# Chunked attention and two feed-forward networks in one kernel: blocks of 512 tokens, attention in quarters of the array, early conversion of the second network's weights

## The chip, the cores and the metric

One core of a Trainium2 chip runs the whole program in one launch. The metric is the device time in microseconds (us), the median of the runs shown. The profile is one execution; its span goes from the first to the last instruction.

## The reference

What is computed, in order (q, k, v have 8 batches, 8 heads, 576 positions, 64 channels; there are 4608 tokens, d_model is 512, d_ff 2048):

```python
# attention inside chunks of 64 positions
scores = q_c @ k_c.T / 8;  attn = exp(scores - max);  attn /= sum(attn) + 1e-9
x  = (attn @ v_c), heads side by side: [4608, 512]
h  = x @ w_in1;   x2  = relu(h)**2 @ w_out1
h  = x2 @ w_in2;  g = (a0 + a1 h + a2 h^2 + a3 h^3) / (1 + |b0||h| + |b1|h^2 + 1e-6)
out = g @ w_out2
```

The four weight matrices come as float64, everything else as float32.

## The kernel before, in words

Tokens run along the free axis. Every float32 operand of the networks is split exactly into two float32r parts, hi and lo, and every product is made of three passes, lo\*hi + hi\*lo + hi\*hi (`mm3`, L159 to L163; L161, L162 and L163 are the three passes). Tokens are cut into 12 blocks of NB = 384, d_ff into 16 chunks of 128. A **step** is one block with one chunk: the product into d_ff (`mm_h`, L165, 12 matrix instructions of 384 columns, into a tile h), the activation, and, LAG = 3 steps later, the product out of that chunk (`mm_out1`, L172, or `mm_out2`, L179) into four accumulators ACC in PSUM. The first network's product out has weights as the stationary operand (12 instructions of 384 columns, named acc<-gh,w and acc<-gl,w in the profile); the second's has the activations as the stationary operand and streams the weights (9 instructions of 512 columns, acc<-w,gh and acc<-w,gl; for the last four chunks acc<-wx,...). The first network's output goes to DRAM (x2d) and comes back for the second.

The first network's activation (`act1`, L200) is Relu and Square on ScalarE, then gh (a copy) and gl (a difference) on VectorE. The second's (`e1` to `e4`, L401 to L441) has six operations on ScalarE, six on VectorE, and gl on GpSimd.

**Attention** works on tiles of 128 tokens with all heads, and is woven into the first network's steps for the block after. Scores (`mm_s`, L276) and outputs (`mm_pv`, L286) are float32 products on halves of the array's columns, two at a time, 8 products of 128 columns (16 instructions in the trace) each. For that KP holds k with zeros for the other head of a pair, and AT the transposed probabilities with zeros for the other chunk. Between them VectorE takes maximum, difference, sum, reciprocal, product (`s_max`, `s_norm`) and one transpose in 32x32 blocks (`s_tr`, L318), whose pieces eight DMAs put into AT. The output leaves PSUM in `x_evac` (L329), a copy on ScalarE and a difference on VectorE. The q and k of the first nine tiles are transposed by TensorE (`tr_nat`), of the others by VectorE (`tr`, L241) from loads of 192 tokens. PSUM holds four accumulators, two h tiles and two tiles a for attention.

**Weights** come as float64 words and are made float32 on the chip (`w_words` on ScalarE, L128; `w_join` and `w_sign` on VectorE, L135 and L140), then split (`w_split`, L145: hi on ScalarE or VectorE, lo on GpSimd). A half is one chunk of one matrix, 128x512. The second network's weights take the slots of the first's when the last block is done with them, so their loads and their conversion lie in that block's steps and in the next.

**The order of the work.** Each event is put down by `at(time, ...)`, with the time in steps, and `issue` (L87) issues them in order of time, so every engine's queue has that order. Up to 14.5 steps the framework's own scheduler may reorder them (`in_order=False`, L554); from there on the order is as written. Each engine works its queue strictly in order. The constants of the order:

```python
n_ahead = 6                                             # L496: w_in halves ahead of the first step
w_get(-1.2 + 0.58 * j, 4.2, w_in1, w_out1, f, half, ...)  # L501: the other 26
start.append(NF * b - 8.6 - (TPB - 1 - i) * NF / TPB)   # L483: attention of tile i of block b
t0 = max(t, t0 + 0.5)                                   # L518: a second-network half every 0.5 step
```

Of the kernel before, what the change touches and what calls it, by code (L numbers as in the profile page):

```python
# [9 lines left out]
F32 = mybir.dt.float32  # L10
F32R = mybir.dt.float32r
# [8 lines left out]
NB = 384          # tokens of a block  # L20
UNIT = 192        # tokens of a load of q and k
LAG = 3           # steps from a product into d_ff to the product out of it
LN_SHIFT = 20     # Ln sees Q * 2**-LN_SHIFT
# [3 lines left out]
def attn_moe_moe_kernel(  # L27
# [37 lines left out]
    NAT = 3 * TPB     # tiles whose q and k the tensor engine transposes  # L65
# [6 lines left out]
    acc_p = ctx.enter_context(tc.tile_pool(name="acc", bufs=1, space=PSUM))  # L72
# [4 lines left out]
    ACC = [acc_p.tile([128, 512], F32, name=f"acc{i}", tag=f"acc{i}") for i in range(4)]  # L77
    x2d = [dram_p.tile([128, KC, NB], F32, name=f"x2d{b}", tag=f"x2d{b}") for b in range(NBLK)]
    co = const.tile([128, 8], F32, name="co")
    P = {}            # pools of the segment that is issued  # L80
    T = {}            # tiles on their way
# [5 lines left out]
    def issue(until, in_order=True):  # L87
        events.sort(key=lambda e: e[:2])
        with tc.manual_schedule() if in_order else nullcontext():
# [505 lines left out]
```

## Time and profile before

| | us |
|---|---|
| median of 3 runs | 1792.72 |
| lowest, highest | 1791.61, 1794.39 |
| profiled execution: span | 1790.2 |
| TensorE matrix instructions busy | 1727.4 (96%) |
| VectorE busy | 1197.0 (67%) |
| ScalarE busy | 1002.2 (56%) |
| GpSimd busy | 376.1 (21%) |
| chain that ended last: TensorE's share | 86% |

The profiled execution's span is 2.5 us below the median of the runs. The span of an instruction on TensorE includes time in its pipeline, so that 0.34 us of one overlaps the next; the distance from start to start is what an instruction costs. DVE is VectorE, ACT ScalarE, POOL GpSimd, SP the queue that issues the DMAs; PEld are the loads of the stationary operand, which overlap PE. A group's name is output<-inputs by the program's tile names.

### The profile page before, as it was taken

The page shows a single profiled execution, that of the slowest core. Times are in us where ns is not written, and L with a number is a line of the kernel's source. Part 1 is how long each engine was busy: PE and PEld are TensorE (multiplying, and loading weights), DVE is VectorE, ACT ScalarE, POOL GpSimd, SP SyncE. Part 2 cuts the span into 40 slices and gives each one's busy share as a digit, 9 for nine tenths or more (in the row PEclk, how much of TensorE's full clock was granted, in tenths as well). Part 3 has the DMA queues.
Part 4 walks back from the last instruction along what each step waited for, and adds up shares of the span by engine and source line. Part 5 has one row for each costly group of instructions (what it writes and reads, how often), then busy time and mean ns, then how long its engine had stood idle before and what let it go on. Part 6 is the DMA issues. An engine that isn't in the chain of part 4 may idle for free.

```text
span 1790.2 us, 26938 instructions
## 1 busy us (share of the span) xinstructions
PE 1727.4 (96%) x9888; PEld 1606.5 (90%) x9888; DVE 1197.0 (67%) x2117; ACT 1002.2 (56%) x1893; POOL 376.1 (21%) x343
## 2 busy tenths in 40 slices
PE   6789999999999999999986999999999999999998
PEld 5689999999999999999976999998989889889887
DVE  6994444444454444544599888888878878887876
ACT  6653222222222222222466888888787888888876
POOL 3540000000000000000386332332332322322322
PEclk9999999999999999999999999999999999999999
DMA  7654132232222322211453010000010000010000
GB/s 186 191 159 83 38 64 53 43 69 49 56 54 43 69 55 48 59 38 42 141 165 128 14 36 25 12 36 24 13 36 24 12 36 24 13 36 18 18 19 18
DMA packets 224484, 100.62 MB, mean 56 GB/s; under 512 B 183136, under 2 KB 214112, under 8 KB 224352
## 3 DMA queue, kind: packets, MB, share of 16 engines
q1 hardware_dynamic: 224352, 98.90, 21.0%
q8 instruction: 78, 1.28, 0.3%
q14 instruction: 54, 0.44, 0.1%
HBM read 71.31 MB, written 18.87 MB: 50 GB/s over the span
## 4 chain that ended last, share of the span: by engine, by line
PE 86%; DVE 8%; issue 4%; ACT 1%; DMA 1%; SPq 0%; POOL 0%; DVEq 0%; POOLq 0%; ACTq 0%
PE h L161 14%; PE acc L161 14%; PE h L162 14%; PE h L163 14%; PE acc L163 13%; PE acc L162 13%; DVE st L137 2%; PE a L283 2%; DVE wc L142 2%; PE a L292 2%; DVE gh L101 1%; DVE t L406 0%; DVE t L426 0%; DVE g L432 0%; DVE ev L101 0%
## 5 line engine op out<-in xcount | busy, mean ns | idle before, releaser
L161 PE MATMUL h<-x,w 128*128 128x384 f32 x1536 | 523.1, 341 | 28.6 <-ACT r L204 19.8
L162 PE MATMUL h<-x,w 128*128 128x384 f32 x1536 | 518.0, 337 | 0.3 <-DVE x L104 0.3
L163 PE MATMUL h<-x,w 128*128 128x384 f32 x1536 | 517.7, 337 | 0.0
L101 DVE CAST gh<-r 128x384 fp32r<-128x384 f32 x192 | 77.5, 404 | 391.1 <-PE acc L163 337.4
L161 PEld LDWEIGHTS h<-x,w 128*128 128x128 f32 x1536 | 290.1, 189 | 47.1 <-ACT r L204 20.9
L204 ACT ACTIVATE r<-h 128x384 f32<-128x384 f32 x192 | 93.7, 488 | 400.6 <-PE h L163 366.9
L104 POOL TENSOR_TENSOR gl<-g,gh 128x384 fp32r<-128x384 f32 x192 | 195.4, 1017 | 566.9 <-ACT gh L99 527.5
L162 PEld LDWEIGHTS h<-x,w 128*128 128x128 f32 x1536 | 290.0, 189 | 9.5 <-DVE x L104 0.7
L163 PEld LDWEIGHTS h<-x,w 128*128 128x128 f32 x1536 | 289.8, 189 | 0.2 <-issue 0.2
L161 PE MATMUL acc<-gh,w 128*128 128x384 f32 x768 | 262.5, 342 | 3.6 <-DVE ev L101 2.1
L163 PE MATMUL acc<-gh,w 128*128 128x384 f32 x768 | 259.2, 337 | 0.0
L162 PE MATMUL acc<-gl,w 128*128 128x384 f32 x768 | 259.0, 337 | 0.0
L406 DVE SCALAR_TENSOR_TENSOR t<-h,co,t 128x384 f32<-128x384 f32 x192 | 139.6, 727 | 124.5 <-ACT t L405 123.0
L104 POOL TENSOR_TENSOR gl<-r,gh 128x384 fp32r<-128x384 f32 x16 | 20.7, 1296 | 761.7 <-DVE gh L101 761.7
L161 PE MATMUL acc<-w,gl 128*128 128x512 f32 x432 | 171.3, 397 | 2.1 <-DVE ev L101 2.1
L162 PE MATMUL acc<-w,gh 128*128 128x512 f32 x432 | 171.0, 396 | 0.0
L163 PE MATMUL acc<-w,gh 128*128 128x512 f32 x432 | 170.7, 395 | 0.0
L161 PEld LDWEIGHTS acc<-gh,w 128*128 128x128 f32 x768 | 144.7, 188 | 10.2 <-issue 5.9
L163 PEld LDWEIGHTS acc<-gh,w 128*128 128x128 f32 x768 | 145.0, 189 | 0.0
L413 ACT ACTIVATE r<-t,co 128x384 f32<-128x384 f32 x192 | 118.6, 618 | 46.7 <-DVE t L406 29.0
L162 PEld LDWEIGHTS acc<-gl,w 128*128 128x128 f32 x768 | 144.6, 188 | 0.0
L99 ACT ACTIVATE gh<-g 128x384 fp32r<-128x384 f32 x192 | 100.9, 525 | 75.4 <-DVE g L432 75.4
(83 smaller groups left out, 2659.5 us busy)
## 6 DMA issues: line engine op xcount, KB each, us to landing
st<-in_moe_w_in_dram SPq DMA_DIRECT2D x32, 512.0 KB, 3.9
st<-in_moe_w_out_dram SPq DMA_DIRECT2D x32, 512.0 KB, 3.7
x2d<-ev SPq DMA_DIRECT2D x48, 192.0 KB, 2.0
x<-x2d SPq DMA_DIRECT2D x12, 768.0 KB, 4.3
out_dram<-ev SPq DMA_DIRECT2D x36, 256.0 KB, 2.0
at<-et SPq DMA_DIRECT2D x264, 32.0 KB, 1.8
v<-in_v_dram SPq DMA_DIRECT2D x32, 256.0 KB, 3.2
qs<-in_q_dram SPq DMA_DIRECT2D x288, 24.0 KB, 1.8
```

The lines of the kernel that those rows point to most:

```text
L99: nc.scalar.activation(out=o, in_=x, func=ACTF.Copy)
L101: eng.tensor_copy(out=o, in_=x)
L104: eng.tensor_tensor(out=o, in0=x, in1=hi.bitcast(F32), op=ALU.subtract)
L137: nc.vector.scalar_tensor_tensor(out=st[:, :, 0], in0=c, scalar=3, in1=st[:, :, 0], op0=ALU.logical_shift_left, op1=ALU.bitwise_or)
L142: nc.vector.scalar_tensor_tensor(out=c, in0=st[:, :, 1], scalar=-2 ** 31, in1=st[:, :, 0], op0=ALU.bitwise_and, op1=ALU.bitwise_or)
L161: nc.tensor.matmul(out=o, lhsT=al, rhs=bh, start=first and i == 0, stop=False)
L162: nc.tensor.matmul(out=o, lhsT=ah, rhs=bl, start=False, stop=False)
L163: nc.tensor.matmul(out=o, lhsT=ah, rhs=bh, start=False, stop=last and i == len(pairs) - 1)
L204: nc.scalar.activation(out=r, in_=ps, func=ACTF.Relu)
L283: nc.tensor.matmul(out=o[sl, p], lhsT=q_[:, p, sl], rhs=k_[:, p, c], start=True, stop=True)
L406: nc.vector.scalar_tensor_tensor(out=t, in0=h2, scalar=co[:, 5:6], in1=t, op0=ALU.mult, op1=ALU.add)
L413: nc.scalar.activation(out=r, in_=u, func=ACTF.Ln, scale=2.0 ** -LN_SHIFT, bias=co[:, 6:7])
```

## The change

Blocks have 512 tokens (nine blocks, four tiles each), so all matrix instructions of the networks have 512 columns, and the second network's w_out chunks all live in W (the wx tiles go). Attention's products work on quarters of the array: 16 products of 64 rows, 64 stationary and 64 moving columns each, in the order of QUARTERS, with each pair of heads in two PSUM banks; KP, AT's zeros and E2 go. In the steady order VectorE's transposes write the transposed probabilities directly, in eight pieces, and no DMA does. TensorE transposes q, k and the probabilities of the first four tiles alone. The second network's weights are converted during blocks 1 to 7, one half per three steps, and kept as float32 in DRAM (w2d); in the last block they are loaded into their slots and split. All is issued in the written order. PSUM first holds h and three double banks for attention, then h, four accumulators and one double bank.

```diff
-NB = 384          # tokens of a block
+NB = 512
...
+    def w_keep(key):
+        _, f, half = key
+        nc.sync.dma_start(out=w2d[f][half], in_=T.pop(("wc",) + key).bitcast(F32))
...
+    def w2_load(f, half):
+        nc.sync.dma_start(out=w_slot(f, half)[1].bitcast(F32), in_=w2d[f][half])
+
+    def w2_split(f, half, eng):
+        hi, lo = w_slot(f, half)
+        x = lo.bitcast(F32)
+        copy(eng, hi, x)
+        split_lo(nc.gpsimd, lo, x, hi)
...
+    QUARTERS = ((0, 0), (1, 1), (0, 1), (1, 0))
...
+    def mm_s(t, tag="a"):
+        q_, k_ = T.pop(("q", t)), T.pop(("k", t))
+        o = banks(P["aps"].tile([128, 2, 512], F32, name="a", tag=tag))
         for p in range(HP):
-            for c in range(2):
-                sl = slice(64 * c, 64 * c + 64)
-                nc.tensor.matmul(out=o[sl, p], lhsT=q_[:, p, sl], rhs=k_[:, p, c], start=True, stop=True)
-        T["s", t] = o.rearrange("p a h j -> p (a h) j")
+            for h, c in QUARTERS:
+                nc.tensor.matmul(out=o[half(c), h, p], lhsT=q_[half(h), p, half(c)], rhs=k_[half(h), p, half(c)],
+                                 start=True, stop=True)
+        T["s", t] = o
...
+            for c, h in QUARTERS:
+                nc.tensor.matmul(out=o[half(h), c, p], lhsT=v_[half(c), 2 * p + h], rhs=a_[half(c), :, p, h],
+                                 start=True, stop=True)
...
-        x = tl("attn", [128, 2, H, 32], F32, "et")
-        nc.vector.transpose(out=x, in_=e.rearrange("p h (a j) -> p a h j", a=2))
+        a = T["a", t] = tl("attn", [128, 2, HP, 2, 32], F32, "at", f"at{t % 2}")
         for c in range(2):
             for ih in range(2):
                 for jh in range(2):
                     i0, j0 = 64 * c + 32 * ih, 64 * c + 32 * jh
-                    nc.sync.dma_start(out=AT[t % 2][j0:j0 + 32, c, ih], in_=x[i0:i0 + 32, jh])
...
+                    nc.vector.transpose(out=a[j0:j0 + 32, ih], in_=e[i0:i0 + 32, :, :, 32 * jh:32 * jh + 32])
...
+    def attention(t, t0):
+        at(t0 - 1.2, tr, t, "qs", "q")
+        at(t0 - 1.0, tr, t, "ks", "k")
+        at(t0 + 0.45, mm_s, t)
+        at(t0 + 0.65, s_max, t)
+        at(t0 + 0.95, s_exp, t)
+        at(t0 + 1.1, s_sum, t)
+        at(t0 + 1.4, s_norm, t, nc.vector)
+        at(t0 + 1.55, s_tr, t)
+        at(t0 + 0.5, load_tok, t, v, "v", f"v{t % 2}")
+        at(t0 + 3.45, mm_pv, t)
+        at(t0 + 3.7, x_evac, t, nc.vector)
...
+        start[t] = 0.5 + 3.6 * i if b == 1 else NF * (b - 1) - 2 + 4 * i
...
+    n_ahead = 4
...
+        w_get(-0.8 + 0.5 * j, 1.3, 0, f, half_, w_split, (nc.scalar, nc.vector)[j % 2])
...
-                at(s + LAG + 0.6 + 0.1 * c, evac1, s // NF, c)
...
+                at(s + LAG + 0.98 + 0.01 * c, evac1, s // NF, c)
+                at(s + LAG + 1.2 + 0.1 * c, store1, s // NF, c)
...
+    for j in range(2 * NF):
+        w_get(NF + 4.2 + 3.0 * j, 3, 1, j // 2, j % 2, w_keep)
     T_P2 = NS - NF - 0.1
...
+    for f in range(NF):
+        for half_, t in ((0, NS - NF + f + 0.6), (1, NS - NF + f + LAG + 0.95)):
+            at(t, w2_load, f, half_)
+            at(t + 2.1, w2_split, f, half_, (nc.scalar, nc.vector)[half_])
```

## Rows read from the trace of the kernel before

**Rows 1.** Stretches: start and end (us), busy us (instructions) by engine, PEclk, DMA share, GB/s

```profile
0.00:35.08 35.08, 21.32 (x152) 15.67 (x152) 19.37 (x35) 20.04 (x35) 12.88 (x23) 0.95 0.78 180
35.08:130.56 95.48, 78.16 (x484) 71.54 (x485) 91.35 (x131) 60.86 (x114) 46.23 (x32) 0.96 0.65 183
...
207.04:281.05 74.01, 74.01 (x482) 71.48 (x481) 34.34 (x70) 20.36 (x40) 0.00 (x0) 1.00 0.26 54
...
871.89:957.00 85.11, 70.37 (x386) 67.77 (x385) 76.38 (x81) 52.97 (x99) 63.26 (x43) 0.98 0.52 170
957.00:1036.50 79.50, 70.52 (x346) 64.00 (x347) 70.01 (x109) 60.02 (x115) 33.62 (x28) 0.96 0.13 46
...
1237.50:1305.00 67.50, 67.24 (x337) 60.60 (x336) 54.33 (x98) 54.36 (x103) 20.17 (x20) 1.00 0.07 24
1710.10:1790.20 80.10, 74.18 (x364) 65.34 (x363) 57.81 (x106) 56.65 (x104) 18.28 (x18) 1.00 0.06 21
```

**Rows 2.** TensorE's timeline in a first-network block, around one burst: start, us, instruction

```profile
634.06 0.34 PE L161 MATMUL acc<-gh,w 128*128 128x384 f32 x1
...
635.97 0.34 PE L163 MATMUL acc<-gh,w 128*128 128x384 f32 x1
636.24 1.09 PE L283 MATMUL a<-kp,q 128*64 128x128 f32 x16
637.26 0.44 PE L161 MATMUL h<-x,w 128*128 128x384 f32 x1
637.54 0.34 PE L162 MATMUL h<-x,w 128*128 128x384 f32 x1
```

**Rows 3.** TensorE's timeline in the second network, two places

```profile
1109.72 0.39 PE L161 MATMUL acc<-wx,gl 128*128 128x512 f32 x1
...
1110.40 0.39 PE L161 MATMUL acc<-wx,gl 128*128 128x512 f32 x1
...
1261.62 0.40 PE L161 MATMUL acc<-w,gl 128*128 128x512 f32 x1
...
1263.02 0.34 PE L161 MATMUL h<-x,w 128*128 128x384 f32 x1
...
1265.13 0.39 PE L161 MATMUL acc<-w,gl 128*128 128x512 f32 x1
```

**Rows 4.** VectorE's groups, 207 to 281 us: shape, count | busy, mean ns | idle before

```profile
L104 DVE TENSOR_TENSOR gl<-r,gh 128x384 fp32r<-128x384 f32 x16 | 8.9, 559 | 0.6
L101 DVE CAST gh<-r 128x384 fp32r<-128x384 f32 x16 | 5.8, 359 | 37.6 <-PE acc L163 33.2 <-ACT ev L99 4.4
...
L322 DVE STREAM_TRANSPOSE et<-e 128x512 f32<-128x512 f32 x3 | 2.1, 702 | 0.0
...
L253 DVE STREAM_TRANSPOSE kp<-ks 64x256 f32<-64x256 f32 x4 | 1.8, 438 | 0.1
```

**Rows 5.** VectorE's groups, 35 to 131 us

```profile
L137 DVE SCALAR_TENSOR_TENSOR st<-wc,st 128x512 int32<-128x512 int32 x28 | 25.4, 906 | 1.0 <-ACT st L131 0.9
L142 DVE SCALAR_TENSOR_TENSOR wc<-st 128x512 int32<-128x512 int32 x28 | 23.9, 855 | 1.1
L101 DVE CAST gh<-r 128x384 fp32r<-128x384 f32 x15 | 14.0, 935 | 0.6 <-ACT r L205 0.6
L104 DVE TENSOR_TENSOR gl<-r,gh 128x384 fp32r<-128x384 f32 x15 | 10.2, 681 | 0.1
L101 DVE CAST w<-wc 128x512 fp32r<-128x512 f32 x13 | 5.5, 423 | 0.2
```

**Rows 6.** VectorE's groups, 872 to 957 us

```profile
L142 DVE SCALAR_TENSOR_TENSOR wc<-st 128x512 int32<-128x512 int32 x25 | 36.3, 1450 | 2.8 <-DVE st L137 0.5
...
L101 DVE CAST w<-wc 128x512 fp32r<-128x512 f32 x11 | 14.4, 1313 | 0.4
```

**Rows 7.** GpSimd's groups, 872 to 957 us

```profile
L104 POOL TENSOR_TENSOR w<-wc,w 128x512 fp32r<-128x512 f32 x21 | 35.6, 1696 | 3.3 <-DVE w L101 3.3
```

More of the change, by code (lines that the diff above doesn't have):

```diff
@@ L1 @@
[L1 removed]
+from contextlib import ExitStack
 import math
@@ L104, in split_lo, with w_slot, w_load @@
         eng.tensor_tensor(out=o, in0=x, in1=hi.bitcast(F32), op=ALU.subtract)
-    def w_load(wi, wo, f, half):
+    def w_slot(f, half):
+        return [W[f][:, p, half * DM:(half + 1) * DM] for p in range(2)]
+    def w_load(n, f, half):
+        wi, wo = ((w_in1, w_out1), (w_in2, w_out2))[n]
         st = tl("w", [128, DM, 2], I32, "st")
@@ L208, in act1, with half @@
         T["g", s] = g
-    KP, AT, E2, own = [], [], [], {}
+    QUARTERS = ((0, 0), (1, 1), (0, 1), (1, 0))
+    def half(i):
+        return slice(64 * i, 64 * i + 64)
     def runs(t0, n):
@@ L258, in tr_nat, with tr @@
-    def tr_nat(t, src, nm, bank):
-        x = T.pop((src, t))
-        o = ACC[bank] if t < TPB + 2 else aps_p.tile([128, 512], F32, name="a", tag="a")
-        o = o.rearrange("p (a b) -> p a b", a=HP)
+                out=T[nm, "unit", u][32 * Q:32 * Q + 32, hp, :n // 32],
+                in_=src[bb, 2 * hp + Q // 2, ss:ss + n, 32 * (Q % 2):32 * (Q % 2) + 32]
+                .rearrange("(t r) d -> r t d", r=32),
+            )
+    def tr(t, nm, o):
+        T[o, t] = tl("attn", [128, HP, 128], F32, o)
+        for u, to, of, n in units(t):
+            nc.vector.transpose(
+                out=T[o, t].rearrange("p a (g r) -> p a g r", r=32)[:, :, to // 32:(to + n) // 32],
+                in_=T[nm, "unit", u][:, :, of // 32:(of + n) // 32, :])
@@ L276, in mm_s, with banks @@
-    def mm_s(t):
-        assert own["k", t % 2] == t
-        q_, k_ = T.pop(("q", t)), KP[t % 2].rearrange("p a h (c j) -> p a c h j", c=2)
-        o = aps_p.tile([128, HP, 2, 64], F32, name="a", tag="a")
+                out=ps[:, p], in_=x[:, 2 * p:2 * p + 2, :].rearrange("p h d -> p (h d)"), identity=P["ident"])
+        T[o, t] = tl("attn", [128, HP, 128], F32, o)
+        copy(nc.scalar, T[o, t], ps)
+    def banks(ps):
+        return ps[:, :, 0:256].rearrange("p a (b j) -> p a b j", j=64)
@@ L286, in mm_pv @@
     def mm_pv(t):
-        assert own["a", t % 2] == t
-        v_, a_ = T.pop(("v", t)), AT[t % 2].rearrange("p c i h r -> p h (c i) r")
-        o = aps_p.tile([128, HP, 128], F32, name="a", tag="a")
-        for h in range(H):
-            sl = slice(64 * (h % 2), 64 * (h % 2) + 64)
-            nc.tensor.matmul(out=o[sl, h // 2], lhsT=v_[:, h], rhs=a_[:, h], start=True, stop=True)
+        v_, a_ = T.pop(("v", t)), T.pop(("a", t))
+        o = banks(P["aps"].tile([128, 2, 512], F32, name="a", tag="a"))
@@ new lines, in f_tr, with f_copy @@
+    def f_tr(t):
+        e = T.pop(("e", t))
+        o = h_p.tile([128, HP, 128], F32, name="h", tag="h")
+        for p in range(HP):
+            nc.tensor.transpose(out=o[:, p], in_=e[:, p].rearrange("p a j -> p (a j)"), identity=P["ident"])
+        T["aT", t] = o
+    def f_copy(t):
+        o = T.pop(("aT", t))
+        a = T["a", t] = tl("attn", [128, 2, HP, 2, 32], F32, "at", f"at{t % 2}")
+        for h in range(2):
+            for c in range(2):
+                copy((nc.scalar, nc.vector)[c], a[half(c), :, :, h].rearrange("p i b r -> p b i r"),
+                     o[half(h), :, half(c)].rearrange("p b (i r) -> p b i r", i=2))
@@ L398, in t2, with x_evac @@
+    def x_evac(t, eng):
+        b, i = divmod(t, TPB)
+        xh, xl = (z[:, :, i * 128:(i + 1) * 128].rearrange("p b (c i) -> p c b i", c=2) for z in X[b % 2])
+        x = T.pop(("x", t))
+        copy(nc.scalar, xh, x)
+        split_lo(eng, xl, x, xh)
     def t2(nm):
@@ new lines, in attention @@
+    def attention(t, t0):
[10 more added lines that the diff above has]
+        at(t0 + 3.7, x_evac, t, nc.vector)
+    start = {}
+    for t in range(TPB, NTILE):
+        b, i = divmod(t, TPB)
+        start[t] = 0.5 + 3.6 * i if b == 1 else NF * (b - 1) - 2 + 4 * i
+        attention(t, start[t])
```

294 lines of the change are left out of this document (100 added, 194 removed).

## The prediction

> **What bounds the kernel now.** I read the stretches by block first (a block here is 16 steps, that is 192 h products), then TensorE's timeline inside one block of each network, then VectorE's groups in the stretches where TensorE has gaps.
>
> The stretches [rows 1] show three regimes. From 207 us on, a first-network block lasts 74.01 us and TensorE is busy for all of it: it is the bound, with VectorE at 34.3 and ScalarE at 20.4. A second-network block lasts 67.50 us, again TensorE's. In between, TensorE has holes: 35.1 us before the first h product; a first block of 95.5 us in which VectorE is busy 91.35; and the two blocks around the change of networks, 85.1 and 79.5 us, in which VectorE works 76.4 and 70.0 us at converting weights. So a part that shortens TensorE's stream counts in full in the long regimes, and a part that unloads VectorE counts in the holes only.
>
> Inside a first-network block [rows 2] eleven matrix instructions of 384 columns start 1.91 us apart, 0.1736 each; 24 of these are the clean step, 4.17 us. A burst of attention (one of two per tile of 128 tokens) costs more than its own length: from the last acc start at 635.97 to the second h start at 637.54 there are 1.57 us where two pitches, 0.35, would do, so 1.22 us. Sixteen clean steps and six bursts make 66.7 + 7.3 = 74.0, the whole block.
>
> In the second network [rows 3] an h instruction of 384 columns takes 0.1758 (12 from 1263.02 to 1265.13); one of 512 that streams a wx tile takes 0.227 (3 in 0.68); one of 512 that streams w takes 0.233 (6 from 1261.62 to 1263.02).
>
> **The change, part by part.** The sum is made against the profiled span of 1790.2 us; the median of the runs shown is 1792.7, so I add 2.5 at the end.
>
> *Blocks of 512.* The columns stay the same; the instructions of 384 become three quarters as many of 512. 0.227 against 4/3 of 0.1736 = 0.2315 says that about 13 ns of each are fixed. A first-network step becomes 24 x 0.2267 = 5.44 us, a clean block 87.05, nine of them 783.4 where twelve of 66.7 were 800: -16. In the second network the products out of d_ff had 512 columns already; they keep 0.2333, since all chunks now stream from w and the wx tiles are gone. The h products get 0.2267 + 0.003, the excess of their 0.1758 scaled up, 0.2296. A step is 12 x (0.2296 + 0.2333) = 5.555, a block 88.9, plus 0.3 for the accumulators' copies at its end (today 0.3 too: 67.50 against 16 x 4.2). Eight such blocks: 713.6. Bounds of the step: 5.44 (everything at the wx pitch) and 5.60 (everything at the w pitch). VectorE and ScalarE, 54.3 and 54.4 us of 67.5 now, grow by at most 4/3, to 72.5 of 89.2: still cover.
>
> *Attention in quarters.* A burst today is 16 matrix instructions of 128 columns on half the array's columns; after it is 32 of 64 columns, four at a time. From the burst's first start to the following product are 1.02 us, and 0.20 more are lost at its edges [rows 2]. 16 x 128 columns of two passes, two at a time, at today's 0.45 ns a column take about 0.9 of the 1.02, 0.11 a pair. Halved, with edges kept, the burst is 0.12 + 0.45 + 0.20 = 0.77. Since 32 instructions and 32 weight loads are issued in place of 16, I take 0.85. No row shows a product of 64 columns or four at a time. The bounds are 0.77; today's 1.22, if rows of the array do not run side by side; and 2.1, if what a pair costs does not shrink with its columns (a rival). There are 64 bursts after against 66 now. Seven blocks with eight bursts: 7 x (87.05 + 6.8) = 657. By the Trainium skill, TensorEngine Tiling (Array Packing), Instruction Overhead, each matmul carries some 60 cycles, and a tiling factor should not be taken from a dimension that is small already. An estimate from it: at 2.4 GHz 32 x 25 ns = 0.80 us for the body, a burst of about 1.1, and 56 x 0.27 = 15 us more in the sum. No row here shows a matmul that short.
>
> *VectorE in those blocks.* The eight copies per tile by DMA (at<-et) go; one whole transpose of 0.70 becomes eight of 32 rows by 256 elements. The nearest row is 64x256 at 0.438 [rows 4]; I take 0.42, 3.4 us per tile (bounds 0.35 and 0.70 each: less than its 128x512 price by size, or all of it). Five whole-tile operations (maximum, subtraction, sum, product, x split) and the transposes of q and k at 0.70 make 4.9, and I allow 0.4 for the two tiny ones of 8 columns: a tile costs 8.7 us. Four tiles 35; 16 activations at 4/3 of (0.359 + 0.559) [rows 4], 19.6; copies 1.4; five and a third early weight halves at 1.4 to 1.8, 9: 65 of 93.9 us. Cover holds, by 29 us a block. The early weights also put 5.3 loads, as many stores and ten ScalarE passes in a block, on SP and ScalarE, which have room (20.4 us of 74). The stores stand on SP ahead of q and k loads, which are issued four steps early.
>
> *One pair of banks for scores and outputs, instead of two tiles.* The next tile's scores now wait on TensorE for the previous tile's x split on VectorE; behind them in TensorE's queue stands that step's acc product. The order leaves 0.75 step, 4 us, for a copy and a split of 1.3 us: nothing, unless VectorE is behind by over 2.7 us (0 to 1.5 us per tile). The stores that now stand in the order by themselves, and join and sign in one event, cost nothing on SP and VectorE while those have this room.
>
> *Start.* Four tiles instead of three must pass before the first h product, but attention now stands ahead of the weights, zero tiles need no clearing, and k needs one copy instead of two. 35.1 now [rows 1]; I take 35 (30 to 42).
>
> *First block.* VectorE binds it now and will. Early prices [rows 5]: join and sign 0.906 + 0.855 per weight half, 0.423 for a hi copy, 0.935 + 0.681 for an activation. Test on the old: 26 halves 45.8, 13 copies 5.5, 14 activations 22.6, three tiles at six operations of 0.70 and small ones 14: 88 us to its fifteenth step, within the 91.35 busy of the whole block. After: 28 halves 49.3, 14 copies 5.9, 15 activations with 0.3 for the longer rows 28.8, four tiles 36, the fifth's first operations 3: 123; 5 of that is done before the first product, and 1.3 steps, 7 us, follow at TensorE's pace: 125. Bounds: 102 with steady prices (0.7 an operation), 152 with those of the change of networks [rows 6]. Against the clean 94 this costs 31, where the old first block lost 95.5 - 74.0 = 21.5.
>
> *Change of networks.* The conversion leaves this place: the last block only copies hi and subtracts lo. Its VectorE load is two operations a step. GpSimd carries two splits a step at 1.70 [rows 7] and the activation's, another 1.7 at most: 5.1 of 5.44, so little cover, and LAG's three steps behind it. I take 87 + 2 = 89 for the last block and nothing for the next, where 85.1 - 66.7 and 79.5 - 67.5 were lost: -30. If GpSimd's cover is gone, 16 x 0.3 = 5 us.
>
> *Last block.* Today 80.1, 12.6 over a plain one; the tail's operations are longer by up to a third, so 88.9 + 14.7 = 103.6.
>
> **Sum.** 35 + 125 + 657 + 89 + 713.6 + 103.6 = 1723.2; plus 2.5: 1725.7 us, 67 less than now.
>
> **The rivals.**
> - *Quarters run, the burst is no shorter* (1.22). In blocks bound by TensorE 56 bursts lose 0.37: 1747. For it: twice the weight loads, and no short product in the trace. Against: today's burst follows its columns.
> - *The opening eats it.* First block 152, first product at 42: 1760. For it: the sign step took 1.45 in the other conversion stretch. Against: GpSimd's share falls, since 28 halves spread over a longer block.
> - *Tiles wait for the single bank pair* or for VectorE's queue, 1.5 us on each of 28 tiles: 1768. Against: 29 us of slack a block.
> - *The early conversion is not hidden:* 32 halves at 1.76 land on the path: 1782. Against: the same slack.
> - *Slower: a pair has a fixed price.* Then 16 pairs at 0.11 cost 1.76, with 0.32 around them 2.1 us a burst, 64 x 1.25 = 80 more: 1806. It decides from 1.9 us a burst. For it: edges of 0.2 us show that changes of mode have fixed costs. Against: 0.11 a pair is what its columns alone take.
>
> **How the numbers follow.** Forecast 0.58 (its own range 1700 to 1745, from the first block's and the step's bounds), no shorter burst 0.13, opening 0.10, bank pair 0.06, conversion 0.05, fixed price 0.08. The range of 1695 to 1775 takes in the first four, and below a first block of 110 with a step of 5.47; the last two and the edges stay out. Runs of this kernel differ by some 0.2%, so 1789 to 1796 counts as the same: 0.03, from conversion and bank pair at their worst. Faster 0.88, slower 0.09.
>
> **What would show it.** h products of 512 columns 0.227 apart in the first network; bursts of x32 under 1 us from edge to edge; blocks of about 94, then 89 at the change with no hole; a first block of about 125 with VectorE over nine tenths busy. I am wrong if first-network blocks exceed 100 us, if the first h product comes after 45 us, or if TensorE waits in its middle blocks on VectorE's x or maximum.

## The result, and the profile after

The changed kernel takes 1809.8 us (1805.1 to 1810.7, four runs), the kernel before 1793.4 beside it: ratio 1.0088, interval 1.0076 to 1.0101. It is slower by nearly a per cent, where I had forecast 67 us less.

From the page of the changed kernel (busy time, share of the span of 1808.9 us and instructions of each engine):

```profile
PE 1704.2 (94%) x9264; PEld 1357.5 (75%) x9264; DVE 1177.0 (65%) x1930; ACT 914.3 (51%) x1476; POOL 345.2 (19%) x270
```

The same stretches as in [rows 1], cut where the first h product of each block starts: the start, the first two blocks, the last first-network block, the first second-network block, a plain one, and the last.

```profile
0.00:49.04 49.04, 22.67 (x305) 17.11 (x305) 23.12 (x42) 21.05 (x39) 9.86 (x14) 0.74 0.66 135
49.04:195.07 146.03, 104.35 (x637) 81.25 (x638) 115.45 (x179) 63.87 (x109) 39.66 (x28) 0.82 0.50 130
195.07:297.95 102.88, 98.63 (x642) 77.78 (x641) 57.45 (x112) 30.24 (x52) 0.00 (x0) 0.97 0.31 78
...
897.55:986.56 89.01, 89.01 (x386) 72.06 (x385) 12.19 (x29) 30.08 (x52) 54.22 (x42) 1.00 0.37 107
986.56:1079.75 93.19, 90.01 (x386) 71.62 (x385) 74.91 (x99) 63.54 (x101) 37.91 (x28) 1.00 0.12 40
1169.00:1258.25 89.25, 88.89 (x386) 71.88 (x384) 68.09 (x100) 65.75 (x103) 25.76 (x20) 1.00 0.07 24
1704.60:1808.90 104.30, 97.89 (x421) 78.20 (x419) 72.64 (x107) 67.03 (x104) 23.28 (x18) 1.00 0.06 21
```

Against the terms of the forecast, with the fastest kernel of the experiments (e13) beside it:

| us | forecast | after | e13 |
|---|---|---|---|
| to the first h product | 35 | 49.0 | 45.9 |
| first block | 125 | 146.0 | 129.6 |
| blocks 1 to 7 | 657 | 702.6 | 675.5 |
| last first-network block | 89 | 89.0 | 89.0 |
| eight second-network blocks | 713.6 | 718.0 | 718.6 |
| last block | 103.6 | 104.3 | 104.4 |
| span | 1723.2 | 1808.9 | 1763.0 |

The second network came out within 5 us of the forecast, and the last first-network block on it. Of the 86 us that the span is over the forecast, 81 lie ahead of that block: 45.6 in blocks 1 to 7, 21 in the first, 14 at the start. Two of the signs of being wrong that I had named are there: a first h product after 45 us, and first-network blocks over 100 us.

**Blocks 1 to 7.** TensorE's waits in them (all seven, 195 to 897 us; us, times, longest):

```profile
PE acc L168 <- ACT ev L98: 21.9, 14, 3.5
PE acc L168 <- DVE ev L100: 2.2, 2, 1.7
```

Two waits a block for ScalarE's copies, and two in all for VectorE's; neither VectorE's x nor its maximum is among them. The accumulators of the block before are not copied out in time. The timeline early in block 2, when block 1's accumulators are copied, says why (start, us, instruction, idle time before it and what ended it; SPq issues the DMAs, x2d<-ev is the store of a copied accumulator, ev its buffer):

```profile
318.88 0.68 DVE L100 COPY ev<-acc 128x512 f32<-128x512 f32 x1
...
319.54 0.58 ACT L98 ACTIVATE ev<-acc 128x512 f32<-128x512 f32 x1
320.14 0.34 SPq L201 DMA_DIRECT2D x2d<-ev  x1
320.17 0.50 PE L168 MATMUL acc<-gh,w 128*128 128x512 f32 x1 [1.05 <-ACT ev L98]
...
321.06 0.61 SPq L201 DMA_DIRECT2D x2d<-ev  x1
...
324.71 0.60 ACT L98 ACTIVATE ev<-acc 128x512 f32<-128x512 f32 x1 [4.59 <-DMA x2d<-ev]
...
325.36 0.80 PE L168 MATMUL acc<-gh,w 128*128 128x512 f32 x1 [3.52 <-ACT ev L98]
325.95 0.63 PE L169 MATMUL acc<-gl,w 128*128 128x512 f32 x1
...
326.38 0.63 PE L170 MATMUL acc<-gh,w 128*128 128x512 f32 x1
...
326.84 0.69 DVE L100 COPY ev<-acc 128x512 f32<-128x512 f32 x1 [7.28 <-DMA x2d<-ev]
...
327.59 0.79 PE L168 MATMUL acc<-gh,w 128*128 128x512 f32 x1 [0.58 <-DVE ev L100]
```

There are two ev buffers and four accumulators. The third copy, ready to go at 320.1, waits 4.6 us until the first store has landed, the fourth 7.3 us for the second. TensorE's queue is in order, so the next block's h products stand behind the acc product that waits. After the wait its instructions start 0.59 and 0.43 us apart instead of 0.23: the granted clock has fallen to the lower of its two levels (0.50 from 325.4 to 330 us). That happens in blocks 1, 2 and 5, which last 102.9 to 103.4 us, with a mean granted clock of 0.97; in the other four, 97.7 to 98.6 us, the waits are shorter (2.5 us a block against 4.3 to 5.2) and the clock stays at 1.00.

**Inside a block**, around one burst (TensorE's timeline, answering to [rows 2]):

```profile
635.39 0.40 PE L168 MATMUL h<-x,w 128*128 128x512 f32 x1
...
637.47 0.39 PE L168 MATMUL h<-x,w 128*128 128x512 f32 x1
...
637.93 0.39 PE L170 MATMUL h<-x,w 128*128 128x512 f32 x1
638.25 0.69 PE L299 MATMUL a<-at,v 64*64 64x64 f32 x32
638.87 0.50 PE L168 MATMUL acc<-gh,w 128*128 128x512 f32 x1
639.21 0.39 PE L169 MATMUL acc<-gl,w 128*128 128x512 f32 x1
...
641.76 0.39 PE L168 MATMUL h<-x,w 128*128 128x512 f32 x1
```

From 637.93 to 639.21 are 1.28 us; less two pitches of 0.23 the burst costs 0.82 (forecast 0.85, before 1.22). Nine instructions in 2.08 us are 0.231 each, not 0.2267. The step, 635.39 to 641.76, is 6.37, and without its burst 5.55 (forecast 5.44).

**The opening.** VectorE's groups in the first block, answering to [rows 5]:

```profile
L135 DVE SCALAR_TENSOR_TENSOR wc<-st 128x512 int32<-128x512 int32 x28 | 33.7, 1203 | 2.9
L133 DVE SCALAR_TENSOR_TENSOR st<-wc,st 128x512 int32<-128x512 int32 x28 | 23.8, 849 | 10.2 <-ACT st L127 10.0
L332 DVE STREAM_TRANSPOSE at<-e 32x256 f32<-32x256 f32 x32 | 13.9, 434 | 0.5
```

Join and sign cost 57.5 us (forecast 49.3), a piece of the transpose 0.434 (0.42). The mean of the sign step, 1.203, hides two prices. VectorE and GpSimd early in the block:

```profile
58.53 0.69 DVE L133 SCALAR_TENSOR_TENSOR st<-wc,st 128x512 int32<-128x512 int32 x1 [2.68 <-ACT st L127]
...
59.09 1.28 POOL L103 TENSOR_TENSOR w<-wc,w 128x512 fp32r<-128x512 f32 x1 [10.53 <-ACT w L98]
...
59.32 1.59 DVE L135 SCALAR_TENSOR_TENSOR wc<-st 128x512 int32<-128x512 int32 x1
```

Of the block's 28 sign steps, the 16 that begin while a split is under way on GpSimd take 1.57 to 1.61 us, the 12 others 0.69. With four joins that meet the same, that is some 18 us over the price alone, and VectorE counts as busy for them.

VectorE is busy for 115.5 of 146 us, 79% where I wanted over nine tenths: it does not bind alone. Other waits of that block, in us, times, longest:

```profile
ACT wc L126 <- DMA st<-in_moe_w_in_dram: 25.0, 10, 8.3
...
PE a L290 <- DVE x L103: 22.4, 3, 9.1
ACT wc L126 <- POOL w L103: 18.5, 9, 4.6
ACT wc L126 <- DMA st<-in_moe_w_out_dram: 17.4, 7, 3.5
```

ScalarE, where a conversion begins, waits 42 us for raw weights (st) and 18.5 for a free buffer of converted ones (wc, which GpSimd's split frees). SP's queue shows one reason for the first (start, us, instruction, count):

```profile
18.89 7.95 SPq L260 DMA_DIRECT2D qs<-in_q_dram  x16
26.93 8.35 SPq L260 DMA_DIRECT2D ks<-in_k_dram  x16
35.40 0.38 SPq L116 DMA_DIRECT2D st<-in_moe_w_in_dram  x1
...
39.93 0.37 SPq L121 DMA_DIRECT2D st<-in_moe_w_out_dram  x1
```

Each small load of q or k holds the queue 0.5 us, and 32 stand in a row ahead of a weight load. The start feels it too. On ScalarE the copy of the fourth tile's probabilities stands behind the conversion of the weights loaded at 39.93:

```profile
44.37 0.66 ACT L126 ACTIVATE wc<-st 128x512 f32<-128x512 f32 x1 [3.58 <-DMA st<-in_moe_w_out_dram]
...
45.47 0.36 ACT L98 ACTIVATE at<-h 64x256 f32<-64x256 f32 x1
```

The other reason for the missing raw weights is in lines of the change that my copy of the diff left out, since the working never spoke of them:

```diff
-        pool(p1, "nat", 3)
-        P["ev"] = P["nat"]
...
+        pool(p1, "w", 2)
+        pool(p1, "wc", 2)
+        pool(p1, "ev", 2)
...
-            pool(p2, "w", 3)
-            pool(p2, "wc", 3)
```

Raw and converted weights have two buffers in the opening, not three, and ev has two where it had a pool of three.

The opening costs TensorE clock as well, which my working never priced. A mean granted clock of 0.82 over the first block's 146 us means 53 us at the lower level, and TensorE is busy for 34 of them, at 0.43 us an instruction instead of 0.23: some 16 us more than at the upper level. In the kernel before only 7 us of that block are at the lower level; in e14 below, with the same number of TensorE's instructions and shorter waits, 20. How much of the 16 is on the path, and not behind waits that would be there anyway, is not shown.

### The profile page after: what moved, and what is told of

It is laid out like the page before. It is cut to its first block, busy times and chain, and to the rows that moved or that the text cites. A ratio compares the mean times of both kernels' runs of the same rounds, so it can differ in the third digit from the quotient of the medians.

```text
span 1808.9 us, 24577 instructions
## 1 busy us (share of the span) xinstructions
PE 1704.2 (94%) x9264; PEld 1357.5 (75%) x9264; DVE 1177.0 (65%) x1930; ACT 914.3 (51%) x1476; POOL 345.2 (19%) x270
## 4 chain that ended last, share of the span: by engine, by line
PE 81%; DVE 7%; DMA 5%; ACT 3%; issue 2%; SPq 1%; POOL 1%; POOLq 0%; DVEq 0%; ACTq 0%
PE acc L168 14%; PE acc L170 13%; PE h L168 13%; PE acc L169 13%; PE h L170 13%; PE h L169 13%; DMA st<-in_moe_w_in_dram 2%; DMA st<-in_moe_w_out_dram 2%; DMA x2d<-ev 1%; PE a L290 1%; PE a L299 1%; ACT ev L98 1%; DVE t L387 1%; DVE t L367 1%; DVE wc L135 1%
## 5 line engine op out<-in xcount | busy, mean ns | idle before, releaser
L168 PE MATMUL h<-x,w 128*128 128x512 f32 x1152 | 458.6, 398 | 6.4 <-ACT r L216 4.6
L169 PE MATMUL h<-x,w 128*128 128x512 f32 x1152 | 454.6, 395 | 6.1 <-DVE x L103 6.1
L170 PE MATMUL h<-x,w 128*128 128x512 f32 x1152 | 454.8, 395 | 0.0
L103 POOL TENSOR_TENSOR gl<-g,gh 128x512 fp32r<-128x512 f32 x144 | 186.6, 1296 | 565.4 <-ACT gh L98 553.5
L168 PEld LDWEIGHTS h<-x,w 128*128 128x128 f32 x1152 | 220.1, 191 | 57.6 <-issue 5.0
L168 PE MATMUL acc<-gh,w 128*128 128x512 f32 x576 | 238.8, 415 | 24.1 <-ACT ev L98 21.9
L169 PEld LDWEIGHTS h<-x,w 128*128 128x128 f32 x1152 | 219.8, 191 | 54.9 <-DVE x L103 6.6
L170 PEld LDWEIGHTS h<-x,w 128*128 128x128 f32 x1152 | 219.5, 191 | 49.6
L170 PE MATMUL acc<-gh,w 128*128 128x512 f32 x576 | 229.9, 399 | 0.0
L169 PE MATMUL acc<-gl,w 128*128 128x512 f32 x576 | 229.2, 398 | 0.0
L170 PE MATMUL acc<-w,gh 128*128 128x512 f32 x576 | 228.0, 396 | 0.0
L169 PE MATMUL acc<-w,gh 128*128 128x512 f32 x576 | 227.4, 395 | 0.0
L367 DVE SCALAR_TENSOR_TENSOR t<-h,co,t 128x512 f32<-128x512 f32 x144 | 125.8, 873 | 155.8 <-ACT t L366 155.8
L168 PEld LDWEIGHTS acc<-w,gl 128*128 128x128 f32 x576 | 108.1, 188 | 39.8 <-DVE ev L100 10.1
L98 ACT ACTIVATE gh<-g 128x512 fp32r<-128x512 f32 x144 | 91.1, 633 | 92.3 <-DVE g L393 92.3
L374 ACT ACTIVATE r<-t,co 128x512 f32<-128x512 f32 x144 | 104.7, 727 | 51.4 <-DVE t L367 45.9
```

The source lines that it names most:

```text
L98: nc.scalar.activation(out=o, in_=x, func=ACTF.Copy)
L103: eng.tensor_tensor(out=o, in0=x, in1=hi.bitcast(F32), op=ALU.subtract)
L168: nc.tensor.matmul(out=o, lhsT=al, rhs=bh, start=first and i == 0, stop=False)
L169: nc.tensor.matmul(out=o, lhsT=ah, rhs=bl, start=False, stop=False)
L170: nc.tensor.matmul(out=o, lhsT=ah, rhs=bh, start=False, stop=last and i == len(pairs) - 1)
L367: nc.vector.scalar_tensor_tensor(out=t, in0=h2, scalar=co[:, 5:6], in1=t, op0=ALU.mult, op1=ALU.add)
```

## The experiments

All ratios are to the kernel before, run on the same chip. In tables, "first h" is the start of the first h product and "block 0" the first block, from the trace.

**e1, four buffers for ev.** The third and fourth copies go to two further tiles.

```diff
-        ev = tl("ev", [128, 512], F32, "ev")
+        ev = tl("ev", [128, 512], F32, "ev") if c < 2 or b >= NBLK - 2 else tl("attn", [128, 512], F32, "ev", f"vx{c % 2}")
```

> The changed kernel, with four buffers instead of two for the accumulators' copies at the end of a first-network block; nothing else moves. In the profile of the changed kernel blocks 1 to 7 last 97.8 to 103.4 us, 702.6 in all, where 16 clean steps of 5.56 and eight bursts of 0.80 make 95.3. Theory: the whole excess, 35 us, is the third copy that waits for the first one's store, and what TensorE loses by its clock after the wait. Then blocks 1 to 7 fall to about 95.5 each and the time from 1809.8 to about 1775. Rival A: the copies are late because VectorE or ScalarE come to them late in their written order, whatever the buffers; then at least 2 us of each block's wait stays and the time is 1795 or more. Rival B: the store is slow because SP stands behind loads of q and k, and with more buffers the same wait appears at another reader; then nothing moves, 1805 to 1810.

Measured: 1782.4 us, 0.9940 (0.9925 to 0.9955): 27 us less than the change, and faster than the kernel before. Blocks 1 to 7 last 675.5 us instead of 702.6, the same 27. TensorE's waits in them and a block's stretch:

```profile
PE acc L168 <- ACT ev L98: 7.3, 7, 1.0
```

```profile
191.57:288.19 96.62, 95.57 (x641) 75.81 (x640) 57.26 (x112) 30.09 (x52) 0.00 (x0) 1.00 0.33 84
```

One wait of 1.0 a block is left, for the first copy, and the clock is granted in full. These seven waits are what the theory's 1775 lacks. Of the 27 us, 16.8 are waits (24.1 less 7.3) and the rest is the clock of blocks 1, 2 and 5. All other kernels below but e2, e3, e4 and e12 have four buffers for ev.

**e2 to e4, the opening's queues and buffers, one at a time on the changed kernel.** e2 brings the q and k of the first three units of tokens by 8 DMAs each instead of 32 (it takes them from other places of q and k, so only its time counts); e3 gives raw weights a third buffer; e4 issues the small loads from ScalarE's queue. The diff has them in this order.

```diff
+        if u < 3:
+            m = HP * n
+            for Q in range(4 if hp == 0 else 0):
+                nc.sync.dma_start(
+                    out=T[nm, "unit", u][32 * Q:32 * Q + 32, :, :n // 32].rearrange("r a t d -> r a (t d)"),
...
-        pool(p1, "w", 2)
+        pool(p1, "w", 3)
...
-            nc.sync.dma_start(
+            (nc.scalar if u < 3 else nc.sync).dma_start(
```

> The changed kernel, with the loads of the first three units of q and k by VectorE's layout (64, 192 and 192 tokens) made by 8 DMAs each instead of 32, of the same bytes in longer pieces. The pieces come from other places of q and k, so the outputs of tiles 4 to 7 are left wrong; everything behind the loads is the same work. Theory: the opening (first h product at 49.0 us, second block's at 195.0 us) is late because SP spends about 0.5 us on each of these DMAs, 96 of them ahead of and between the loads of weights. With 72 fewer, 36 us of SP's time are free: first h product at 36 to 40 us, second block's at 160 to 170, time about 1780. Rival A: two buffers for the raw weights set the pace (a load waits for the conversion two halves before); then the first h product comes earlier but the first block stays at 135 us or more: 1795 to 1800. Rival B: VectorE's work sets the pace, as predicted; then the first block stays near 140 us too, with VectorE over nine tenths busy, which in the changed kernel it is not.

> The changed kernel, with three buffers instead of two for the raw weights; the room comes from the accumulators' copies, which take two tiles of the opening that are free by then, still two. Theory (SP's issue of q and k loads is the opening's limit): the loads of weights stand in the same order behind the same DMAs, so the opening gains 8 us at most, time 1802 to 1810. Rival A (two raw buffers' turnaround): a load no longer waits for the conversion two halves before, the first block falls from 146 to 120 to 130 us, time 1785 to 1793.

> The changed kernel, with the same 96 small DMAs of q and k issued from ScalarE's queue instead of SP's. ScalarE is busy 4 to 5 tenths of the opening. Theory (SP's issue time): weights' loads go out when their buffers are free; ScalarE pays for the 96 issues with about as much of its own time, so the opening gains less than with fewer DMAs: first h product at 40 to 46 us, second block's at 170 to 185, time 1785 to 1800. Rival A (two raw buffers): second block's at 190 or later, since ScalarE's conversion passes now stand behind the issues as well: 1805 or more. Rival B (the DMAs' own bandwidth): no change beyond 5 us.

| | us | ratio (interval) | first h | block 0 |
|---|---|---|---|---|
| change | 1809.8 | 1.0088 (1.0076 to 1.0101) | 49.0 | 146.0 |
| e2 | 1797.3 | 1.0021 (1.0012 to 1.0031) | 43.5 | 138.0 |
| e3 | 1801.1 | 1.0046 (1.0031 to 1.0061) | 48.7 | 138.6 |
| e4 | 1825.4 | 1.0181 (1.0166 to 1.0196) | 71.7 | 137.4 |

The small loads cost 13 us where they stand (e2), and the missing raw buffer some 9 (e3). Neither makes up the opening: e2 came out as its rival A had it, e3 just past its theory's 8 us and far from its rival's 17 or more. Moving the loads to another engine's queue also shortens the first block by 9, but ScalarE starts no operation while it issues, and the first product comes 23 us later, as e4's rival A had it (ScalarE's timeline of e4: sixteen issues, then the copy that attention waits for):

```profile
27.11 9.35 ACTq L260 DMA_DIRECT2D ks<-in_k_dram  x16
36.51 0.38 ACT L98 ACTIVATE at<-h 64x256 f32<-64x256 f32 x1 [10.10 <-DMA ks<-in_k_dram]
```

**e5 to e8, parts of the opening on top of e1.** e5 takes work from VectorE: all hi copies of the opening's weights go to ScalarE, the first block's gl to GpSimd. e6 loads q and k of tiles 4 to 7 in their natural layout and transposes them on TensorE, so that the small loads there go. e7 adds the third raw buffer and loads 1.8 steps ahead instead of 1.3. e8 is all three. Of e5, then e6:

```diff
-        split_lo(nc.gpsimd if s >= NS - NF else nc.vector, g[1], r, g[0])
+        split_lo(nc.gpsimd if s >= NS - NF or s < NF else nc.vector, g[1], r, g[0])
...
-        w_get(-0.8 + 0.5 * j, 1.3, 0, f, half_, w_split, (nc.scalar, nc.vector)[j % 2])
+        w_get(-0.8 + 0.5 * j, 1.3, 0, f, half_, w_split, nc.scalar)
...
+        if t < 2 * TPB:
...
+            at(t0 - 0.46, tr_nat, t, "qn", "q")
```

> The kernel of e1 (four buffers; first h product at 48.3 us, first block 143.3 us, time 1782.4), with two things taken from VectorE in the first block: all hi copies of the weights on ScalarE (14 of 0.42 us) and the activation's differences on GpSimd (16 of about 0.75 us), 18 us of the 117 it is busy there. Theory (the prediction's: VectorE's work sets the first block): the block falls by 15 us or more, to 128 or less, time 1765 to 1768. Rival (no engine is full; the engines wait for each other in the written order, for raw weights and for the single bank pair): less than 8 us, time 1775 to 1785; slower if GpSimd's 28 splits and the differences stand in each other's way.

> The kernel of e1, with q and k of tiles 4 to 7 loaded in natural order by one DMA each (two where a tile crosses a batch) and transposed by TensorE, as tiles 0 to 3 are, in place of 96 small loads and VectorE's transposes; the small loads begin with tile 8. Outputs are whole. Theory (SP's issue of small loads delays the weights): as in e2, first h product at 40 to 44 us, and since VectorE loses 6 us as well, the first block at 125 to 135: time 1762 to 1770. Rival (the pace of raw weights alone): first h product earlier, first block at 137 or more, time 1773 or more.

> The kernel of e1, with a third buffer for raw weights in the opening, loads issued half a step earlier. The room is the tile whose halves serve the accumulators' copies later. Theory (turnaround of two raw buffers): e3 gained 7 us with three buffers at the old distance; here 10 to 15 us, first block 128 to 134, time 1767 to 1773. Rival (SP's order): as in e3 or less, time 1774 or more.

> e1 and the edits of e5, e6 and e7 together. If SP's issue, raw buffers and VectorE each hold the opening in turn, the gains add to more than each alone: first h product at 40 to 43 us, first block at 105 to 118, time 1735 to 1752. If one common cause is behind all three, the sum is no more than the largest of them: 1765 or more.

| | us | ratio (interval) | first h | block 0 |
|---|---|---|---|---|
| e1 | 1782.4 | 0.9940 (0.9925 to 0.9955) | 48.3 | 143.3 |
| e5 | 1779.1 | 0.9920 (0.9900 to 0.9941) | 48.7 | 140.6 |
| e6 | 1776.2 | 0.9904 (0.9882 to 0.9926) | 43.4 | 142.1 |
| e7 | 1774.5 | 0.9895 (0.9870 to 0.9919) | 46.1 | 136.6 |
| e8 | 1772.0 | 0.9887 (0.9868 to 0.9905) | 45.8 | 136.6 |

One by one they take 3, 6 and 8 us off e1, together 10: they do not add up, so something they share was still in the way. e5's 3 us are within the intervals of the two, and e6's 6 hardly outside. All four times lie where the rival had them, not the theory. The waits of e7's first block suggest the next limit, the two converted buffers:

```profile
ACT wc L128 <- POOL w L103: 34.8, 19, 5.7
```

**e9, the halves of W apart.** A test of the pitch: each half of W in a tile of its own, as the wx tiles were, which streamed at 0.227 [rows 3].

```diff
-    W = [const.tile([128, 2, 2 * DM], F32R, name=f"w{f}") for f in range(NF)]
+    W = [[const.tile([128, 2, DM], F32R, name=f"w{f}_{i}") for i in range(2)] for f in range(NF)]
```

> The kernel of e1 with the two halves of each chunk of weights (w_in and w_out) in tiles of their own, [128, 2, 512] each, as the wx tiles of the kernel before were; nothing else. In the kernel before a 512-column product that streamed wx took 0.227 us from start to start, one that streamed w 0.233. Theory: the distance between hi and lo (or the width of the tile) sets this, and the second network's step falls from 5.53 to about 5.45: 1.3 us a block, time 1770. Rival: it is something else about these products; the step stays at 5.53, time 1780 to 1784.

Measured: 1783.3 us, 0.9951 (0.9936 to 0.9967), against e1's 0.9940. Second-network blocks stay at 89.2 us, first-network ones at 96.6. How the halves lie in their tile is not what sets the pitch. In this trace the first block takes 148.4 us against e1's 143.3, with nothing of its order changed: if that is scatter from one execution to the next, a difference of 2 to 5 us between two block 0 values below says little by itself.

**e10 to e12, the converted buffers.** e10 gives converted weights four buffers on top of e7; e11 adds e6's loads to that; e12 takes the kernel *before* and gives it the two raw and two converted buffers of the change. Of e10, then e12:

```diff
+        own = key[0] == 0 and T["m"] >= 4 and T["m"] % 4 >= 2
+        c = tl("attn", [128, DM], I32, "wc", f"vx{T['m'] % 2}") if own else tl("wc", [128, DM], I32, "wc")
...
-            pool(p2, "w", 3)
-            pool(p2, "wc", 3)
+            pool(p2, "w", 2)
+            pool(p2, "wc", 2)
```

> The kernel of e7 (first h product at 46.1 us, first block 136.6, time 1774.5) with four buffers instead of two for the converted weights in the opening, from two tiles that attention no longer needs by then. Each half holds its buffer through two operations on ScalarE, two on VectorE, the hi copy and GpSimd's difference, some 5 us, and in e7 ScalarE waits 35 us in all for GpSimd to give one back. Theory (the ring of buffers sets the pace of the opening): the first block falls to 110 to 122, time 1750 to 1762. Rival (attention of tiles 4 to 7 and its single bank pair hold the first block, whatever the weights do): 130 or more, time 1768 or more.

> The kernel of e10 with the natural loads of e6 as well. Theory (buffers first, SP's small loads second): first h product at 42 to 44 us and first block 105 to 118, time 1742 to 1755. Rival: the natural loads gain their 4 us of start and nothing in the block, as between e7 and e8: 1765 or more if e10's block stays at 130.

> The kernel before with two buffers instead of three for raw and for converted weights in its opening, nothing else. There the opening (up to 14.5 steps) is ordered by the framework's scheduler. Theory (the number of buffers sets the pace of the opening): its first block, 95.5 us, becomes 110 to 120, and its time 1807 to 1817. Rival (VectorE's work sets it, busy 91 of 95.5 us): within 5 us of before, 1790 to 1798.

e10: 1774.7 us, 0.9898 (0.9879 to 0.9918), the same as e7. The wait for converted buffers is gone, and TensorE's on VectorE's x has grown from 15.7 us to 18.4; VectorE is busy for 115.3 of 139.1. e11: 1770.5, 0.9877 (0.9861 to 0.9894). Both are where the rival had them. e12: 1823.7, 1.0172 (1.0151 to 1.0192), 31 us slower than the kernel before. Its first two blocks, and TensorE's longest wait in the first:

```profile
35.02:148.79 113.77, 84.86 (x467) 75.46 (x466) 78.63 (x126) 61.73 (x114) 39.51 (x30) 0.91 0.55 154
148.79:237.32 88.53, 78.40 (x497) 75.44 (x497) 35.18 (x70) 23.90 (x47) 2.59 (x2) 0.94 0.25 53
```

```profile
PE acc L161 <- POOL w L104: 16.6, 11, 3.8
```

Against 95.5 and 76.5 before, with VectorE busy for 78.6 of 113.8 instead of 91.35 of 95.5 [rows 1]: with two buffers TensorE waits for weights while VectorE stands idle part of the time. The first block is as the theory had it, and the second loses 12 more. So a loss of that size comes with the buffers, without attention in quarters or blocks of 512. It is not shown to be theirs alone: the scheduler, which orders this opening, also made another order for the smaller pools (TensorE's instructions differ after the first 100, VectorE's after the first 31).

**e13 to e15, what is left.** e13 is e11 with e5's relief of VectorE; e14 is e13 with the small loads back; e15 is e11 with the x split of tiles 4 to 7 put ahead in VectorE's order. Of e15:

```diff
-        at(t0 + 3.7, x_evac, t, nc.vector)
+        at(t0 + (3.46 if t < 2 * TPB else 3.7), x_evac, t, nc.vector)
```

> The kernel of e11 (three raw, four converted buffers, natural loads for tiles 4 to 7; first block 135.2 us, time 1770.5) with VectorE's relief of e5: hi copies of the first network's weights on ScalarE, the activation's differences of the first block on GpSimd, together some 18 us less of VectorE's 111. Theory (three limits near each other in the first block: the buffers' ring, SP's order, VectorE's work; with the first two widened VectorE is the one that TensorE waits for, through x's split and the single bank pair): the block falls to 108 to 122, time 1745 to 1758. Rival A (the engines' waits on each other in the written order cost the same whoever is relieved): 130 or more, 1765 or more. Rival B: ScalarE or GpSimd becomes the one waited for, and the block gets longer.

> The kernel of e13 without the natural loads, so SP issues 96 small loads in the opening again and VectorE transposes q and k of tiles 4 to 7. Theory: SP's order is one of the three limits, so the block is some 8 us longer than in e13 and the time 8 to 14 us more. Rival: once the buffers are wide, SP's order costs nothing; within 4 us of e13.

> The kernel of e11 with one change of order: for tiles 4 to 7 the copy and split of attention's output stand right behind its product (3.46 steps after the tile's start instead of 3.70), ahead of an activation and a conversion on VectorE and ScalarE. Theory (TensorE waits for x's split through the single bank pair, since VectorE runs late): each of three waits shortens by 2 to 3 us, first block 126 to 130, time 1761 to 1766. Rival (the time lost moves to the next thing VectorE owes): within 3 us of e11, 1768 to 1773.

| | us | ratio (interval) | first h | block 0 |
|---|---|---|---|---|
| e11 | 1770.5 | 0.9877 (0.9861 to 0.9894) | 45.8 | 135.2 |
| e13 | 1763.4 | 0.9835 (0.9819 to 0.9852) | 45.9 | 129.6 |
| e14 | 1765.2 | 0.9846 (0.9826 to 0.9866) | 46.7 | 129.2 |
| e15 | 1772.0 | 0.9884 (0.9864 to 0.9904) | 45.8 | 138.4 |

e13 is the fastest kernel of the study, 1.65% under the kernel before; it falls between its theory (at most 122 and 1758) and its rival A (from 130 and 1765). VectorE's relief gave 3 us with narrow buffers (e5) and gives 7 with wide ones, and four converted buffers, which gave nothing in e10, give 9 once VectorE is relieved (e8 against e13): in these pairs each counts only with the other. Once both are there, the small loads cost nothing that can be told apart (e14).

Putting the x split first does not help (e15), but that says nothing of its place, since e11's TensorE has no wait for VectorE's x to shorten. In all kernels with the natural loads (e6, e8, e11, e13, e15) that wait at the single bank pair is gone, and TensorE's transposes, which write into h tiles, wait for ScalarE to read an earlier h. The largest of these in the first block, of e11 and of e13:

```profile
PE h L289 <- ACT r L228: 11.3, 2, 8.3
```

```profile
PE h L289 <- ACT r L228: 11.7, 3, 7.0
```

With the small loads TensorE still waits for VectorE's x, 22 us in e14. So the natural loads trade one wait for another.

The start is four tiles in turn (TensorE's timeline of e13, the second part of each tile's output product, then the first h product):

```profile
16.74 1.12 PE L311 MATMUL a<-at,v 64*64 64x64 f32 x30 [1.88 <-DVE at L100]
...
26.29 1.12 PE L311 MATMUL a<-at,v 64*64 64x64 f32 x30 [0.86 <-DVE at L100]
...
35.84 1.13 PE L311 MATMUL a<-at,v 64*64 64x64 f32 x30 [0.85 <-DVE at L100]
...
42.15 1.13 PE L311 MATMUL a<-at,v 64*64 64x64 f32 x30 [0.85 <-DVE at L100]
45.86 0.79 PE L173 MATMUL h<-x,w 128*128 128x512 f32 x1 [2.59 <-ACT x L98]
```

## Why the prediction was wrong, and where it was right

**The step that failed most plainly** is, in my words, "The stores that now stand in the order by themselves, and join and sign in one event, cost nothing on SP and VectorE while those have this room". I asked whether the queues had room, not how many buffers the stores hold. With two buffers the third accumulator's copy waits for a DMA, at the end of each of blocks 0 to 6, with TensorE behind it: 27 us, shown by e1, which adds buffers and changes nothing else. The change had put a copy behind a transfer, and my working named no one who waits for it.

**"First block. VectorE binds it now and will."** The work was nearly right (115 us busy, where the sum has 123 less the 5 done before the block) and the conclusion wrong: VectorE is busy for 79% of the block. Some 18 us of that work are steps that met a split on GpSimd; the rows that I took hold a smaller share of this (0.855 a sign step, where 0.69 is the price alone). The test on the old kernel, 88 us against 91 busy, came out well because VectorE ran there almost without a break. I took that density over as a property of VectorE. e12 shows that it hung on the buffers, with the order that the scheduler makes for them: take one of each kind away from the kernel before, and 31 us come on top with VectorE idle a third of the first block. In the changed kernel several limits lie close together: the raw buffer (8 to 9 us, e3 and e7), the small loads on SP (13 us with the start, e2), the converted buffers and VectorE (7 to 9, e13 against e11 and e8). They do not add up, and how the 21 us divide among them and the clock is not shown. e13's 129.6 stands 4.6 over the forecast 125, but with work moved off VectorE, so it does not confirm that sum.

**"Start ... I take 35 (30 to 42)"**: 49.0. I counted the tile that comes on top and then set it off against small savings. In e13's rows the tiles pass one after another, the first three 9.55 us apart (the order, `z = 4.7 * t`, had them 4.7 apart) and the fourth 6.3 behind, and the h product stands 10.8 us later than before. That leaves 3.2 for what the changed kernel adds: there the fourth tile's copy on ScalarE comes only at 45.47, for the reason shown above. That the old kernel let its scheduler reorder the start, and the new one issues it as written, is in the front matter and was in none of my steps. What holds the tiles 9.55 us apart, and whether an interleaved order gets the fourth tile's time back, is open.

**"0.227 against 4/3 of 0.1736 = 0.2315 says that about 13 ns of each are fixed."** The first network's instructions cost 0.2315 on average, exactly the 4/3: 24 x 0.2315 = 5.56 where I took 5.44, 0.12 a step or 13.4 us in blocks 1 to 7. The step lay inside its bounds (5.44 to 5.60), but both pitches stood in [rows 3], and I took the smaller for all of the first network from three instructions. The second network, where I kept both, was right: 89.25 a block against 89.2. What makes an instruction of 512 columns take 0.227 or 0.235 is open; e9 rules out the layout of W's halves.

With the fix of e1, blocks 1 to 7 add up: 16 x 5.56 + 8 x 0.82 = 95.5, and 1.0 for the wait that is left, 96.5 against 96.6 in the trace. So the 45.6 us there are 27 for the buffers, 13.4 for the pitch and 7 for the wait that is left, a term I did not have, less 1.7 for bursts that are shorter than forecast. The first second-network block, where I forecast no loss, is 4 us over a plain one; of that the waits for the accumulators' copies (1.4 + 0.8) and for the fresh weights (1.0) make three quarters.

**The rivals.** The one that ended on the slower side, a fixed price for a pair in the array, is refuted though the result lies on its side: a burst costs 0.82 and not 2.1. Nor was the burst as long as before. The Trainium skill, TensorEngine Tiling (Array Packing), Instruction Overhead, would have 32 x 25 ns = 0.80 us for the body of a burst, by an estimate from its 60 cycles at 2.4 GHz; the trace has 0.62 from the burst's start to the next product. For products on four quarters, then, this overhead is not paid in full by each. The opening did eat much, but not for the reason I gave that rival (the sign step at 1.45: it took 1.20). The single bank pair costs nothing in blocks 1 to 7; in the first block TensorE's wait for x shows there, 22.4 us.

**Right**: the burst (0.85 for 0.82), the change of networks (85.1 - 66.7 and most of 79.5 - 67.5 regained), the second network's blocks, the last block, VectorE's cover in the steady blocks (57 to 59 of 103 busy, forecast 65), and the early conversion being hidden there. That the last first-network block met its 89 is partly luck: TensorE is busy for all of its 89.01 us, which are 16 steps at the longer pitch, and the 2 us that I added for GpSimd did not come (54.2 us busy, 3.4 a step where I had 5.1).

## What to carry to other kernels

Count the buffers of every pool that a change touches as you count its instructions: a pool cut from three to two can turn a transfer that was hidden into a wait, first for the engine that fills it and then for the in-order queue behind. Where one engine is busy for nine tenths of a stretch, find out what keeps it fed before taking its work as the bound of the new order. And when several limits lie close, an edit that helps little alone (VectorE's relief, 3 us) can help once the others are gone (7 us), so judge it again at the end; and look first whether the wait that it is to shorten is in the trace of the kernel it goes into (e15).

## What the hardware showed that I had not expected

- A burst of 32 instructions of 64 columns on quarters (16 products) takes 0.62 us to the next product, 19 ns an instruction.
- A DMA of q or k on SP's queue holds it some 0.5 us: 16 in 7.95 us. In e2, with four times the bytes in each, four took 1.74 to 2.62 us, so it is the number that counts. ScalarE's queue is no faster (16 in 9.35), and ScalarE starts nothing meanwhile.
- A sign step on VectorE takes 0.69 us alone and 1.57 to 1.61 when a split on GpSimd has begun before it (16 of 28 in the first block). A join that begins 0.56 us ahead of a split keeps its 0.69. That agrees with the Trainium skill, SBUF — State Buffer, "SBUF: two separate sides", by which a VectorE operation with two inputs from SBUF and a GpSimd one that reads SBUF lock each other out, and the one that starts first goes through. e5 and e13, which move gl to GpSimd, keep the sign step's mean near that of the change (1.301 and 1.167 against 1.203).
